# A fused retention and two-layer MLP kernel: a shorter path for the decay factors, and a new order of the opening

## The chip, the cores and the metric

The kernel runs on one core of a Trainium2 chip. The metric is the device time of one execution in microseconds (us); the kernel before takes 575.96 us, the median of three runs (574.5 to 576.0). The core has five engines that run side by side, each with its own queue in program order: TensorE (PE), which multiplies matrices into PSUM, VectorE (DVE), ScalarE (ACT), GpSimd (POOL) and SyncE (SP), which here issues most of the DMAs. TensorE has its own row for weight loads (PEld). On-chip memory is SBUF, 128 partitions wide; PSUM has 8 banks, and a bank holds one 128x512 float32 tile.

## The reference

Inputs are q, k, v of shape 2 x 8 x 768 x 64 (batch, heads, positions, head size), one decay factor lam for each of the 8 heads, and five weight matrices. The first part is a retention (linear attention with decay), here with all of it in one formula for a chunk of positions b:

```
intra = ((q_b k_b^T) * lam^(i-j) for j <= i, else 0) @ v_b
inter = (q_b * lam^(i+1)) @ state
out_b = intra + inter
state = lam^n * state + (k_b * lam^(n-1-j))^T @ v_b        # n positions in a chunk
```

Its result, as 1536 tokens x 512, goes through a first MLP (`h = x @ w_in`, `g = relu(h)^2`, `g @ w_out`, width 2048) and a second one (`gate = sigmoid(x @ w_gate)`, `val = x @ w_val`, `(gate * val) @ w_out`, width 1536). All of it is float32.

## The kernel before

The kernel takes chunks of 128 positions: chunks 0 to 5 are those of the first sequence, 6 to 11 those of the second, and `PAIRS` (line 22) couples chunk n with chunk n + 6. A pair needs these steps: `att_scores` (L368, 8 small float32 matmuls that show as 16 instructions) for each chunk; `att_mask` (L423, DVE), which multiplies the scores by the decay mask `D`; `query` (L376, POOL), which multiplies q by the rows `L` of decay powers; `att_keys` (L384, POOL) or `keys_by_act` (L392, ACT), which scale k by the column `W`; `att_out` (L463 with the state, L475 with the values); `att_uv` (L447), the product of keys and values, and `att_state` (L487, L489), which adds it to the state `S`; `decayed` (L429, POOL) is the state times `G`. For chunks 0 and 6 the scaled keys are made another way: `turn_keys` (L402) transposes the loaded k on TensorE with the identity matrix `same`, and `turned_keys` (L412, DVE) scales the result.

`decays` (L271 to L318) builds the factors at the start. lam comes by one DMA that writes the 8 values to all 128 partitions (L269, on the SP queue). DVE and ACT spread it to 512 columns (L296), two scans on DVE (L298) make `D`, and `W` follows (L302). `rows(r)` multiplies `D` by a column on TensorE so that its last row stands in all partitions (L311), and ACT copies the result to `L` (L316). `decay_of_state` (L320) makes `G` on POOL. Before the first real matmul, `warm_up(14)` (L331) runs 14 matmuls of 128x512 on zeros.

The MLP matmuls need each float32 operand as a high and a low part, so a weight goes through a chain: load (L139, SP), two scalings on ACT (L153, L157, the word "a" of the plan), shift and add on DVE (L164, L169, "j"), high part by ACT ("h") or DVE ("H", both L230), low part on DVE (L237, "l"). `stage_a` (L538, 12 matmuls) makes h for one f of 16, `elem` and `split_g` (ACT L569, L570, L582, and DVE L584, "g") work on it, `stage_b` (L552, 12 matmuls) multiplies by w_out.

The order of the work is written out by hand. `OPENING` (line 18) is a list of words, one call each, from the scores of chunk 0 to the scores, outputs and states of the first two pairs; the numbers are chunks, and for o and u pairs (R rows, T turned keys, d their scaling, s scores, m mask, q query, K keys, x copy of the result to its high part, z its low part on DVE, o output, u state product, y state, t decayed state). Then `step_1(f)` runs for f = 0 to 15: stage_a(f), stage_b(f - 1), with the letters of `PLAN[f]` between them. Each step has two halves, half 2f after stage_a(f) and half 2f + 1 after stage_b(f - 1); `SLOTS` (line 24) says at which half the scores and outputs of pairs 2 to 5 run on TensorE, and `LOADS` (line 25) at which half the SP queue issues the loads of their q, k and v. Later stages (second MLP, store) are not touched by the change.

Of the kernel before, what the change touches and what calls it, by code (L numbers as in the profile page):

```python
# [12 lines left out]
P = 128  # L13
CH = 128
TB = 512
WARM = 14
SINGLE = 10
OPENING = "R0 T0 s0 R1 m0 q7 s6 q1 q8 T6 m6 d6 a d0 j o0 u0 x0 s1 s7 y K7 x6 m1 h m7 K1 G t z0 l o1 a x1 x7 z6 z7 j a z1 H l j H u1 l".split()
PLAN = ('ga|ajhjlaHl', '|jagajHlH', 'aljg|hjH', '|llqgKmkaj', 'Hqlaa|jhlg', 'jmq|gamKhlajmqj', 'Hmklg|aj', 'aghl|mKakm', 'jhq|aqjglq', 'jhml|gamjqajhm', 'mgla|jh', 'gl|hhlhm', 'lgl|', 'g|', 'g|', '|g')
# [4 lines left out]
SLOTS = ((7, 'scores', 2), (8, 'scores', 8), (10, 'out', 2), (11, 'scores', 3), (12, 'scores', 9), (14, 'out', 3), (16, 'scores', 4), (17, 'scores', 10), (19, 'out', 4), (20, 'scores', 5), (21, 'scores', 11), (23, 'out', 5))  # L24
LOADS = {10: 'v9 v3', 4: 'q2 q9', 20: 'v11', 5: 'q3 q10', 17: 'q5 q12 v5', 1: 'v2 v8', 12: 'v4 q11 q4 v10'}
# [7 lines left out]
def retention_moe_kernel(  # L33
# [80 lines left out]
    def load_kv(c, eng=nc.sync):  # L114
        t = kv_t[c] = double("kv")
        n = c in PAIRS[0]
        eng.dma_start(out=t[:, n:], in_=kv[c, :, n:].rearrange("s t h d -> s t (h d)"))
# [132 lines left out]
    lam8 = const.tile([P, H, 1], F32, name="lam8")  # L250
    seen = const.tile([P, 1], F32, name="seen")
    W = const.tile([P, H, 1], F32, name="W")
    lam_half = const.tile([P, 2, 4, 1], F32, name="lam_half")
# [3 lines left out]
    G = const.tile([P, 2, 4, 1], F32, name="G")  # L257
# [9 lines left out]
    def load_lam():  # L267
        src = bass.AP(lam.tensor, lam.offset, [[0, P], [1, H]])
        nc.sync.dma_start(out=lam8[:, :, 0], in_=src)  # L269

    def decays():  # L271
# [4 lines left out]

        nc.vector.memset(warm, 0.0)
# [9 lines left out]
        nc.vector.tensor_scalar(  # L287
# [5 lines left out]
        )  # L293
        lam_r = pairs_of(lam8)
        for r, copy in enumerate((nc.vector.tensor_copy, nc.scalar.copy)):
            copy(step_d[:, r, :, 1:], lam_r[:, r].to_broadcast([P, 4, CH - 1]))  # L296
        for r in range(2):
# [4 lines left out]
        nc.vector.tensor_tensor(  # L302
            out=pairs_of(W), in0=lam_r, in1=D[:, :, :, CH - 1 :], op=ALU.mult
        )
        last = spot_d[:, 0, 0, 0:1].to_broadcast([P, 64])
        row_t = [bank(), bank()]

        def rows(r):

            for s in range(2):  # L310
                nc.tensor.matmul(  # L311
                    row_t[s][half(r ^ s)], lhsT=last, rhs=D[:, r], start=True, stop=True
                )
            if r:
                for s in (1, 0):
# [1087 lines left out]
```

## Time and profile before

| | |
|---|---|
| median of 3 runs | 575.96 us (574.5 to 576.0) |
| profiled execution, its own time | 574.55 us |
| its span, first to last instruction | 572.4 us |
| TensorE busy | 567.6 us, 99% of the span |
| DVE, ACT, POOL busy | 442.0, 350.3, 53.2 us |
| mean DMA rate | 262 GB/s |
| chain that ended last | PE 98%, DVE 1% |

The profile is of one execution, taken by the hardware profiler; its times are counted from the span's start. Busy shares of TensorE are modelled, so the chain of waits and the start times of the matmuls say more than they do. A view by lines names the line of the kernel, the engine, the operation and its tiles ("out<-in"); "xN" is the count of instructions.

### The profile page before, as it was taken

To read this page: it belongs to the slowest core of one execution; us is meant where nothing else is said; L and a number is where in the kernel's file an instruction comes from. 1 tells how busy PE (TensorE), PEld (TensorE's weight loads), DVE (VectorE), ACT (ScalarE), POOL (GpSimd) and SP (SyncE) were. 2 spreads that over 40 slices of the span, in tenths; PEclk is the share of its full clock that TensorE was granted. 3 is DMA by queue.
4 is the path that set the end of the run, shared out by engine and by line. 5 is a ranking of instruction groups with operands and counts; after the bars stand their busy time and mean duration, and the time that the engine had idled before them with its cause. 6 is when DMAs were issued, how large, how long until landed. Compare 5 with 4: busy or idle time off the path is not lost.

```text
span 572.4 us, 8640 instructions
## 1 busy us (share of the span) xinstructions
PE 567.6 (99%) x3050; PEld 464.2 (81%) x3050; DVE 442.0 (77%) x653; ACT 350.3 (61%) x569; POOL 53.2 (9%) x54
## 2 busy tenths in 40 slices
PE   9999999999999999999999999999999999999997
PEld 5878788888888888888888888888888888888885
DVE  5998887967788867765656778884778887789966
ACT  3688898867565467674648565544555555475552
POOL 3313613000000000000000000120011112000110
PEclk9999999999999999999999999999999999999999
DMA  8999998211454499999985899983546669599681
GB/s 305 407 407 413 408 352 302 93 38 37 148 183 148 148 360 347 408 412 409 405 322 187 304 342 346 370 261 71 159 84 171 225 193 252 189 345 340 212 289 74
DMA packets 68843, 149.74 MB, mean 262 GB/s; under 512 B 6976, under 2 KB 15168, under 8 KB 68800
## 3 DMA queue, kind: packets, MB, share of 16 engines
q1 hardware_dynamic: 64448, 141.59, 67.6%
q0 software_dynamic: 3840, 6.69, 6.0%
q10 hardware_dynamic: 512, 0.92, 0.5%
q8 instruction: 24, 0.39, 0.3%
q14 instruction: 19, 0.16, 0.1%
HBM read 105.39 MB, written 42.21 MB: 258 GB/s over the span
## 4 chain that ended last, share of the span: by engine, by line
PE 98%; DVE 1%; DVEq 0%; issue 0%
PE p L747 33%; PE p L538 19%; PE p L1145 15%; PE p L552 14%; PE p L1074 10%; PE p L368 2%; PE p L475 2%; PE p L331 1%; PE p L447 1%; PE p L463 1%; DVE xl L507 0%; DVE at L423 0%; PE p L311 0%; PE p L402 0%; DVE wlo L237 0%; DVE j L169 0%
## 5 line engine op out<-in xcount | busy, mean ns | idle before, releaser
L747 PE MATMUL p<-xch,ah 128*128 128x512 f32 x280 | 109.1, 390 | 0.0
L747 PE MATMUL p<-xcl,ah 128*128 128x512 f32 x280 | 109.0, 389 | 0.0
L747 PE MATMUL p<-xch,al 128*128 128x512 f32 x280 | 108.9, 389 | 0.0
L757 ACT COPY s<-p 128x512 f32<-128x512 f32 x60 | 35.2, 586 | 68.3 <-PE p L747 68.3
L747 PEld LDWEIGHTS p<-xch,ah 128*128 128x128 f32 x280 | 52.5, 188 | 11.3 <-ACT s L757 0.3
L747 PEld LDWEIGHTS p<-xch,al 128*128 128x128 f32 x280 | 52.6, 188 | 11.0
L747 PEld LDWEIGHTS p<-xcl,ah 128*128 128x128 f32 x280 | 52.6, 188 | 10.9
L1074 PE MATMUL p<-gq,wq 128*128 128x512 f32 x252 | 57.5, 390 | 0.0
L1074 PEld LDWEIGHTS p<-gq,wq 128*128 128x128 f32 x252 | 47.2, 188 | 10.1 <-DVE wq L1031 0.3
L169 DVE CUSTOM_DVE_ANT_0 j<-j,r 128x1024 uint16<-128x1024 uint16 (+1 forms) x57 | 46.6, 817 | 5.8
L1145 PE MATMUL p<-g2h,whi 128*128 128x512 f32 x128 | 49.8, 389 | 0.0
L1145 PE MATMUL p<-g2l,whi 128*128 128x512 f32 x128 | 49.8, 389 | 0.0
L1145 PE MATMUL p<-g2h,wlo 128*128 128x512 f32 x128 | 49.8, 389 | 0.0
L153 ACT ACTIVATE j<-raw 128x512 f32<-128x512 f32 x68 | 45.7, 672 | 5.9 <-DMA raw<-in_w 2.0
L157 ACT ACTIVATE r<-raw 128x512 int32<-128x512 uint32 x68 | 45.3, 666 | 1.5 <-PE p L538 1.0
L762 DVE TENSOR_TENSOR c<-p,s 128x512 f32<-128x512 f32 x60 | 41.2, 687 | 5.7 <-PE p L747 4.1
L538 PE MATMUL p<-xh,whi 128*128 128x512 f32 x160 | 43.7, 395 | 0.0
L538 PE MATMUL p<-xl,whi 128*128 128x512 f32 x160 | 42.9, 390 | 0.1
L538 PE MATMUL p<-xh,wlo 128*128 128x512 f32 x160 | 43.0, 390 | 0.0
L695 POOL DMA_DIRECT2D as<-w x6 | 5.6, 928 | 354.6 <-DMA u<-w 278.6
L538 PEld LDWEIGHTS p<-xl,whi 128*128 128x128 f32 x160 | 30.0, 188 | 6.8 <-DVE xl L507 0.5
L538 PEld LDWEIGHTS p<-xh,wlo 128*128 128x128 f32 x160 | 30.0, 188 | 6.6 <-DVE wlo L237 0.3
(133 smaller groups left out, 1027.1 us busy)
## 6 DMA issues: line engine op xcount, KB each, us to landing
raw<-in_w SPq DMA_DIRECT2D x68, 512.0 KB, 7.6
w<-j SPq DMA_DIRECT2D x68, 256.0 KB, 7.1
u<-w SPq DMA_DIRECT2D x52, 256.0 KB, 5.5
a<-w SPq DMA_DIRECT2D x20, 512.0 KB, 4.1
g<-g SPq DMA_DIRECT2D x32, 256.0 KB, 4.0
g<-g SPq DMA_DIRECT2D x16, 512.0 KB, 7.6
gr<-gs SPq DMA_DIRECT2D x24, 256.0 KB, 5.3
qk<-in_qk SPq DMA_DIRECT2D x11, 512.0 KB, 7.7
```

The costliest lines, as they stand in the source:

```text
L153: lambda: nc.scalar.activation(j, t[:, :, 1].bitcast(F32), AF.Prelu, scale=2.0**-80 if flip else 2.0**-112, alpha=2.0**-32 if flip else 2. ...
L157: lambda: nc.scalar.activation(r, low, AF.Copy, scale=2.0**-29),
L169: nc.vector.tensor_tensor(out=j, in0=j, in1=r, op=ALU.add)
L368: nc.tensor.matmul(pv(sc[g])[:, p, :], lhsT=pv(t[:, 1, :])[half(g), p, :], rhs=pv(t[:, 0, :])[half(g), p, :], start=True, stop=True,)
L475: nc.tensor.matmul(ov[s][half(r), p, :], lhsT=v[:, 2 * p + r, :], rhs=pv(at[:, r ^ s, :])[:, p, :], start=n == 0 and p == 0, stop=p == 3, ...
L538: nc.tensor.matmul(acc, lhsT=a[:, kk * P : (kk + 1) * P], rhs=b[:, kk, :], start=i == 0, stop=i == 11,)
L552: nc.tensor.matmul(acc[e], lhsT=a[:, e * P : (e + 1) * P], rhs=b, start=first and i == 0, stop=last and i == 2,)
L747: nc.tensor.matmul(acc, lhsT=w[:, col, kk * P : (kk + 1) * P], rhs=x[:, kk, :], start=start and i == 0, stop=stop and i == 5, skip_group_c ...
L757: nc.scalar.copy(s, acc)
L762: nc.vector.tensor_tensor(out=c, in0=acc, in1=s, op=ALU.add)
L1074: nc.tensor.matmul(acc[k], lhsT=a[:, wn], rhs=block_of(b, gn), start=first and n == 0, stop=last and n == 3 * len(group) - 1,)
L1145: nc.tensor.matmul(acc[e, t], lhsT=a[:, e * P : (e + 1) * P], rhs=b[:, t, :], start=first and i == 0, stop=last and i == 2,)
```

## The change

lam is loaded as one row of 8 values by the ACT queue (before the load of q and k of chunk 6), while the load of q and k of chunk 0 becomes the first of the SP queue. A matmul with a column of ones spreads the row over the partitions into a PSUM bank, and DVE copies it from there. The warm-up is split: 4 matmuls before that small matmul, 5 behind it. `same` is made on POOL. The matmuls of `rows` and the ACT copies are gone; POOL builds `L` by doubling: it copies lam to column 0 and then, in seven steps, multiplies the n columns that exist by the n-th to get n more. `G` is the last column of `L`, so `decay_of_state` is gone; `W` is copied from `D`. In the opening the words stand in a new order, and in the loads v0 comes ahead of q7 and the second weight ahead of v1 and v7. In `SLOTS` the two chunks of a pair have their scores at one half for pairs 2, 4 and 5, and those of chunk 3 stand behind the outputs of pair 2 (12 halves with attention work become 8), and `LOADS` has four places where it had seven. In `out_now` the outputs come ahead of the state products. In `PLAN` three high parts move from ACT to DVE (9 h and 9 H for 12 and 6), and one scaling of keys from POOL to ACT (4 k and 2 K for 3 and 3).

```diff
--- before.py
+++ after.py
@@ -13,16 +13,16 @@
 P = 128
 CH = 128
 TB = 512
-WARM = 14
+WARM = 4, 5
 SINGLE = 10
-OPENING = "R0 T0 s0 R1 m0 q7 s6 q1 q8 T6 m6 d6 a d0 j o0 u0 x0 s1 s7 y K7 x6 m1 h m7 K1 G t z0 l o1 a x1 x7 z6 z7 j a z1 H l j H u1 l".split()
-PLAN = ('ga|ajhjlaHl', '|jagajHlH', 'aljg|hjH', '|llqgKmkaj', 'Hqlaa|jhlg', 'jmq|gamKhlajmqj', 'Hmklg|aj', 'aghl|mKakm', 'jhq|aqjglq', 'jhml|gamjqajhm', 'mgla|jh', 'gl|hhlhm', 'lgl|', 'g|', 'g|', '|g')
+OPENING = "s0 q1 a T0 m0 q7 q8 s6 T6 m6 d6 s1 K1 o0 d0 j K7 x6 u0 s7 y x0 m1 m7 o1 h a l t x1 x7 z6 a z0 z7 z1 j H l j H u1 l".split()
+PLAN = ('g|ajajahlH', '|ljgajHlaa', 'Hjlh|gjHl', '|lgamjqKHak', 'a|ljgHqlq', 'gjm|mmhklmaa', 'jHlkq|agjj', 'h|lamKag', 'mhjjgl|kHajqqq', 'lm|hgamaqmmh', 'jjaHgl|', 'jgl|lhmhll', 'g|', 'g|', 'g|', '|g')
 QUERIES = (2, 9, 3, 10, 4, 11, 5, 12)
 
 PAIRS = ((0, 6), (1, 7), (2, 8), (3, 9), (4, 10), (5, 11))
 LEAD = 2
-SLOTS = ((7, 'scores', 2), (8, 'scores', 8), (10, 'out', 2), (11, 'scores', 3), (12, 'scores', 9), (14, 'out', 3), (16, 'scores', 4), (17, 'scores', 10), (19, 'out', 4), (20, 'scores', 5), (21, 'scores', 11), (23, 'out', 5))
-LOADS = {10: 'v9 v3', 4: 'q2 q9', 20: 'v11', 5: 'q3 q10', 17: 'q5 q12 v5', 1: 'v2 v8', 12: 'v4 q11 q4 v10'}
+SLOTS = ((7, 'scores', 2), (7, 'scores', 8), (10, 'out', 2), (10, 'scores', 3), (11, 'scores', 9), (14, 'out', 3), (15, 'scores', 4), (15, 'scores', 10), (18, 'out', 4), (19, 'scores', 5), (19, 'scores', 11), (22, 'out', 5))
+LOADS = {13: 'v4 q11 q4 v10', 3: 'v2 v8 q2 q9', 8: 'q3 q10 v9 v3', 16: 'q5 q12 v5 v11'}
 
 MM = 0.2267
 SCORES = 1.0
@@ -113,7 +113,7 @@
 
     def load_kv(c, eng=nc.sync):
         t = kv_t[c] = double("kv")
-        n = c in PAIRS[0]
+        n = f"T{c}" in OPENING
         eng.dma_start(out=t[:, n:], in_=kv[c, :, n:].rearrange("s t h d -> s t (h d)"))
 
 
@@ -248,13 +248,13 @@
 
 
     lam8 = const.tile([P, H, 1], F32, name="lam8")
+    lam_row = const.tile([1, H], F32, name="lam_row")
+    ones = const.tile([1, P], F32, name="ones")
     seen = const.tile([P, 1], F32, name="seen")
     W = const.tile([P, H, 1], F32, name="W")
-    lam_half = const.tile([P, 2, 4, 1], F32, name="lam_half")
     warm = const.tile([P, P], mybir.dt.bfloat16, name="warm")
     D = const.tile([P, 2, 4, CH], F32, name="D")
     L = const.tile([P, 2, 4, CH], F32, name="L")
-    G = const.tile([P, 2, 4, 1], F32, name="G")
     same = const.tile([P, P], F32, name="same")
     S = const.tile([P, 2, 4, 64], F32, name="S")
 
@@ -265,8 +265,14 @@
         return t.rearrange("a (p r) o -> a r p o", r=2)
 
     def load_lam():
-        src = bass.AP(lam.tensor, lam.offset, [[0, P], [1, H]])
-        nc.sync.dma_start(out=lam8[:, :, 0], in_=src)
+        src = bass.AP(lam.tensor, lam.offset, [[0, 1], [1, H]])
+        nc.scalar.dma_start(out=lam_row, in_=src)
+
+    def spread_lam():
+
+        t = bank()
+        nc.tensor.matmul(t[:, 0:H], lhsT=ones, rhs=lam_row, start=True, stop=True)
+        nc.vector.tensor_copy(lam8[:, :, 0], t[:, 0:H])
 
     def decays():
 
@@ -274,6 +280,7 @@
 
 
 
+        nc.vector.memset(ones, 1.0)
         nc.vector.memset(warm, 0.0)
         step_d, spot_d = (
             double(name).rearrange("a r (p b) -> a r p b", p=4) for name in ("step_d", "spot_d")
@@ -284,13 +291,16 @@
         nc.gpsimd.iota(across, pattern=[[1, P]], base=0, channel_multiplier=-1)
         nc.scalar.copy(seen, warm[:, 0:1])
         nc.vector.memset(step_d[:, :, :, 0:1], 0.0)
-        nc.vector.tensor_scalar(
+        nc.gpsimd.tensor_scalar(
             out=same, in0=across, scalar1=0.0, scalar2=None, op0=ALU.is_equal
         )
         nc.vector.tensor_scalar(
             out=spot_d.rearrange("a r p b -> a (r p) b"), in0=shift,
             scalar1=float(CH - 1), scalar2=None, op0=ALU.is_equal,
         )
+        warm_up(WARM[0])
+        spread_lam()
+        warm_up(WARM[1])
         lam_r = pairs_of(lam8)
         for r, copy in enumerate((nc.vector.tensor_copy, nc.scalar.copy)):
             copy(step_d[:, r, :, 1:], lam_r[:, r].to_broadcast([P, 4, CH - 1]))
@@ -299,30 +309,23 @@
                 *(t[:, r].rearrange("a p b -> a (p b)") for t in (D, step_d, spot_d)),
                 initial=0.0, op0=ALU.mult, op1=ALU.add,
             )
-        nc.vector.tensor_tensor(
-            out=pairs_of(W), in0=lam_r, in1=D[:, :, :, CH - 1 :], op=ALU.mult
-        )
-        last = spot_d[:, 0, 0, 0:1].to_broadcast([P, 64])
-        row_t = [bank(), bank()]
-
-        def rows(r):
-
-            for s in range(2):
-                nc.tensor.matmul(
-                    row_t[s][half(r ^ s)], lhsT=last, rhs=D[:, r], start=True, stop=True
-                )
-            if r:
-                for s in (1, 0):
-                    nc.scalar.copy(L[:, s].rearrange("a p b -> a (p b)"), row_t[s])
-
-        return rows
-
-    def decay_of_state():
+        nc.vector.tensor_copy(pairs_of(W), D[:, :, :, CH - 1 :])
+
+    def rows():
+
+
+
         lam_r = pairs_of(lam8)
-        nc.gpsimd.tensor_copy(lam_half[half(0)], lam_r[half(0)])
+        nc.gpsimd.tensor_copy(L[half(0), :, :, 0:1], lam_r[half(0)])
         for s in range(2):
-            nc.gpsimd.tensor_copy(lam_half[half(1), s], lam_r[half(1), 1 - s])
-        nc.gpsimd.tensor_tensor(out=G, in0=lam_half, in1=L[:, :, :, CH - 1 :], op=ALU.mult)
+            nc.gpsimd.tensor_copy(L[half(1), s, :, 0:1], lam_r[half(1), 1 - s])
+        n = 1
+        while n < CH:
+            nc.gpsimd.tensor_tensor(
+                out=L[:, :, :, n : 2 * n], in0=L[:, :, :, 0:n],
+                in1=L[:, :, :, n - 1 : n].to_broadcast([P, 2, 4, n]), op=ALU.mult,
+            )
+            n *= 2
 
     def warm_up(n):
 
@@ -428,7 +431,8 @@
         t = unit("tt")
         eng.tensor_tensor(
             out=t.rearrange("a (n e) -> a n e", n=8), in0=S.rearrange("a s p e -> a (s p) e"),
-            in1=G.rearrange("a s p o -> a (s p) o").to_broadcast([P, 8, 64]), op=ALU.mult,
+            in1=L[:, :, :, CH - 1 :].rearrange("a s p o -> a (s p) o").to_broadcast([P, 8, 64]),
+            op=ALU.mult,
         )
         tt_t.append(t)
 
@@ -1175,8 +1179,8 @@
         pair = PAIRS[k]
         if k < SEQ_CH - 1:
             decayed()
+        att_out(pair)
         att_uv(pair)
-        att_out(pair)
         passed(REST)
 
         def after():
@@ -1200,13 +1204,13 @@
         "h": lambda: couple_high(nc.scalar.copy), "H": lambda: couple_high(nc.vector.tensor_copy),
         "l": couple_low, "q": lambda: query(queries.pop(0)),
         "k": lambda: keys_by_act(keys_left.pop(0)), "K": lambda: att_keys(keys_left.pop(0)),
-        "G": decay_of_state, "t": decayed, "y": att_state,
+        "t": decayed, "y": att_state,
     }
 
-    def opening(rows):
+    def opening():
         one = {
-            "R": rows, "s": att_scores, "T": turn_keys, "d": turned_keys, "q": query,
-            "m": att_mask, "K": att_keys, "x": att_x, "z": low_x,
+            "s": att_scores, "T": turn_keys, "d": turned_keys, "q": query,
+            "m": att_mask, "K": att_keys, "k": keys_by_act, "x": att_x, "z": low_x,
             "o": lambda n: att_out(PAIRS[n]), "u": lambda n: att_uv(PAIRS[n]),
         }
         for what in OPENING:
@@ -1269,13 +1273,14 @@
     T5 = T4 + (12 + 42 * NF2) * MM
 
     with tc.manual_schedule():
+        load("q0")
         load_lam()
         load("q6", nc.scalar)
-        load("q0 q7 v0 w q1 v6 q8 v1 v7 w w w w w")
-        rows = decays()
-        warm_up(WARM)
+        load("v0 q7 q1 w v6 q8 w v1 v7 w w w w")
+        decays()
+        rows()
         new_xr()
-        opening(rows)
+        opening()
         clock[0] = 0.0
         flush()
```

## Rows read from the trace of the kernel before

**Rows 1.** Chain of waits in order of time, opening to 46 us: start us, us, what.

```profile
0.99 5.37 PE p L331 x14
6.36 1.01 PE p L311 x4
...
27.21 2.72 PE p L552 x12
29.93 3.03 PE p L538 x12
...
41.14 1.09 PE p L368 x16
42.23 2.95 PE p L538 x12
```

**Rows 2.** Timeline, all engines, 0 to 22 us: start, duration, engine, line, idle before.

```profile
3.56 0.42 DVE L296 COPY step_d<-lam 128x508 f32<-128x508 f32 x1 [0.67 <-DMA lam<-in_lam]
4.02 2.34 DVE L298 TENSOR_TENSOR_SCAN D<-step_d,spot_d 128x512 f32<-128x512 f32 x2
7.30 1.11 PE L402 MATMUL p<-same,qk 64*128 64x64 f32 x16
11.08 3.75 POOL L376 TENSOR_TENSOR qd<-qk,L 128x512 f32<-128x512 f32 x3 [9.05 <-ACT L L316]
15.56 2.28 POOL L384 TENSOR_TENSOR kd<-kv,W 128x512 f32<-128x512 f32 x2 [0.74 <-DMA kv<-in_kv]
17.21 1.10 PE L463 MATMUL p<-qd,S 64*64 64x128 f32 x32
17.79 0.18 POOL L322 COPY lam_half<-lam 64x8 f32<-64x8 f32 x1
17.98 0.69 ACT L153 ACTIVATE j<-raw 128x512 f32<-128x512 f32 x1 [1.05 <-DMA raw<-in_w]
18.41 0.21 POOL L325 TENSOR_TENSOR G<-lam_half,L 128x8 f32<-128x8 f32 x1
21.08 1.20 PE L538 MATMUL p<-xh,whi 128*128 128x512 f32 x4
```

**Rows 3.** Waits from 0 to 30 us: who waited for whom, us, times, longest.

```profile
PEld p L538 <- DVE xl L507: 0.5, 1, 0.5
```

**Rows 4.** DMA issues of 1.17 to 1.61 us: count, KB each, us to landing.

```profile
qk<-in_qk SPq DMA_DIRECT2D x1, 512.0 KB, 5.1
```

**Rows 5.** DMA packets of the window 1.1 to 3.5 us.

```profile
DMA packets 177, 0.14 MB, mean 58 GB/s; under 512 B 144, under 2 KB 144, under 8 KB 177
```

**Rows 6.** Windows of 1 us: length, busy by engine, TensorE clock, DMA share, GB/s.

```profile
5.00:6.00 1.00, 1.00 (x6) 0.35 (x3) 1.00 (x2) 0.00 (x0) 0.00 (x0) 1.00 0.99 393
```

**Rows 7.** Timeline of 23 to 33 us, ACT and PE.

```profile
24.52 0.60 ACT L569 ACTIVATE r<-p 128x512 f32<-128x512 f32 x1 [2.54 <-PE p L538]
...
26.35 0.67 ACT L153 ACTIVATE j<-raw 128x512 f32<-128x512 f32 x1
...
27.50 0.66 ACT L153 ACTIVATE j<-raw 128x512 f32<-128x512 f32 x1
...
29.05 0.63 ACT L230 CAST whi<-j 128x512 fp32r<-128x512 f32 x1 [0.33 <-DVE j L169]
...
32.79 1.09 PE L552 MATMUL p<-gh,whi 128*128 128x512 f32 x4
```

**Rows 8.** Windows of 5 us, columns as in group 6.

```profile
30.00:35.00 5.00, 5.00 (x22) 3.78 (x22) 4.69 (x10) 4.94 (x10) 0.00 (x0) 1.00 1.02 407
```

**Rows 9.** Timeline of 41 to 48 us: ACT and DVE.

```profile
41.36 2.02 ACT L392 ACTIVATE kd<-kv,W 128x64 f32<-128x64 f32 x8 [0.74 <-DMA w<-j]
...
47.13 1.41 DVE L230 CAST whi<-j 128x512 fp32r<-128x512 f32 x1
```

**Rows 10.** DMA issues of 35 to 40 us, and SP's own waits from 20 to 130 us.

```profile
qk<-in_qk SPq DMA_DIRECT2D x2, 512.0 KB, 8.3
...
SPq L117 <- ACT r L157: 4.8, 1, 4.8
```

## The prediction

> **What bounds the kernel now.** I read the page first: TensorE is 99% of the chain, so only three things can move the time: when TensorE starts its dense work, how much work it has, and where it waits. The chain in order of time shows where it is not dense [rows 1]. It begins with 14 warm-up matmuls (0.99 us, 5.37 long), then small float32 matmuls in a row, then a stretch led by DVE, and from 23.3 us on nothing but PE pieces, 2.72 us for 12 matmuls (0.227 each). In that stretch there is one slow group of 12 (3.03 instead of 2.72, at 29.93) and an extra 0.23 us wherever 12 matmuls follow a piece of attention (2.95 instead of 2.72, at 42.23). The timeline of the opening comes next [rows 2]: what was TensorE, or its operands, late for? Last come the waits [rows 3]: 0.5 us for the low part of x is the only one on weights of the main matmuls.
>
> So the time is the start of the first main matmul (21.08 us, rows 2), plus fixed work behind it, plus a few gaps. The profiled execution took 574.55 us, span 572.4, so 2.15 lie around the span. It is the fastest of the shown runs but for rounding: their median is 1.41 above it.
>
> **Term 1, the start of the dense work.** The rows matmuls go: two groups of four, 1.01 us each [rows 1], 2.02 us. The spread of lam adds one tiny matmul (its nearest row is 0.25 us, a quarter of such a group; it lies inside the warm-up). The 14 warm-ups take 5.37 us, 0.38 each, so 9 take 3.5; the wait for lam stands between them. Here lam, a broadcast to 128 partitions, landed at about 3.5: the copy at 3.56 waited for it [rows 2]. As one row at the head of another queue it lands no later than that and after its issue (about 1.1); with this broadcast the nearest row, I take 2.8. The five later warm-ups then end at about 5.0, and D comes as before, at 6.4 (copy 0.42, scans 2.34, rows 2, begun about 0.1 earlier, less the new copy).
>
> The next matmuls are the scores of chunk 0, which need q0 and not D. In the kernel before q0 landed at 1.18 + 5.1 = 6.3 [rows 4]. Ahead of it on the same queue stood lam's small packets: 144 packets below 512 bytes from 1.1 to 3.5 us, in which all queues moved 58 GB/s [rows 5]; later the same engines moved 393 GB/s [rows 6]. Now q0 is first: at best 512 KB at 393 GB/s from 2.0 us on, 3.4; at worst it is only issued 0.44 earlier (0.74 for 1.18) and lands at 5.8. I take 4.8, so these scores begin at 5.3.
>
> From there the same matmuls as before run to the first main one: before from 7.30 to 21.08 with one rows group inside, 13.78 - 1.01 = 12.77 us without a wait [rows 1, 2]. So 5.3 + 12.77 = 18.1, if data keeps up. D at 6.4 is not late: the mask of chunk 0 is wanted by the first output, which stands behind five of these pieces of about 1 us, at 10.
>
> L is next late? The doubling is three copies (0.18 each) and seven products. The 128x8 product took 0.21 and the 128x512 one 1.28 at most [rows 2], so 1.65 to 2.1 ns an element: 7 x 0.2 + 1016 elements x 1.65 to 2.1 = 3.1 to 3.5, with the copies 3.6 to 4.0. L is there at 7.4 instead of 11, and the three queries (1.25 each, 3.75 in all) end by 11.2, or by 13.2 should q8 land late; the state part of output 1 wants them at 14.2 (before it began 21.08 - 17.21 = 3.9 us ahead of the first main matmul, rows 2). Hidden; without that cover it is 4 us.
>
> The loads decide. v1 and v7 have a weight more ahead of them (512 KB, 1.3 us at 393 GB/s). v7 landed at 15.5: POOL waited for it until 15.56 [rows 2]. The queue starts between 0.4 us earlier (the issue) and 1.5 (lam's packets gone from 2.0 to 3.5), I take 1.0, so v7 lands at 15.8, its scaled keys are ready at 17.0 (1.14 each, rows 2), and the last state product (1.1, as the other groups of small matmuls) ends at 18.1. Both paths meet; I take 18.5, between 17.8 and 20.2. The gain is 21.08 - 18.5 = 2.6 us, between 0.9 and 3.3.
>
> **Term 2, from there to the second MLP group.** Before, the L552 group of f = 1 began 32.79 - 21.08 = 11.71 us after the first main matmul [rows 2, 7]. Now the plan puts three "a" ahead of the high part of weight 4. Counted from the first main matmul: relu at 3.04 (the third group of four begins at 1.81, and relu came 1.23 behind it), 1.83 to the first "a", three at 1.15, the high part 0.63 [rows 7]: 8.95, then 12 matmuls, 2.72: 11.67. The two small waits go (0.5 for the low part of x, 0.31 for that of a weight) and one of 0.8 us (8.95 less three groups of 12, 8.16) for a high part comes. Sum: 0.0, between -0.4 and +0.8.
>
> **Term 3, fewer changes of kind.** Attention stands at 8 places instead of 12. Each place costs the 12 matmuls behind it 0.23 us [rows 1]. That is 4 x 0.23 = 0.9, which I take; if the cost comes with each piece and not with each place, it is 0. That outputs now stand ahead of state products moves no work.
>
> **Term 4, the conversions at a faster pace.** From 30 to 35 us ACT is busy 4.94 and DVE 4.69 of 5.00 us [rows 8]: TensorE 2.6 us earlier wants its weights 2.6 us earlier. They start earlier too (the copies of L on ACT are gone, and the masks come with the scores, 2 us sooner). In the plan ACT gains one scaling of keys (2.02, rows 9) and gives up three high parts (0.63 or, of two weights, twice that), about even; DVE takes these, and a DVE cast beside a POOL product took 1.41 us [rows 9]. TensorE's gaps from that lie between 0 and 2.5 us; I take 0.6.
>
> **Sum.** -2.6 + 0.0 - 0.9 + 0.6 = -2.9: 571.65 us against the profiled execution. The shown median is 1.41 above that execution and one run of three is at it, so I put 1.0 on top: **572.6 us**.
>
> **Rivals.**
> *The opening waits for data.* The weight that landed behind v7 came 2.4 us after it (ACT waited until 17.98, rows 2), not 1.3. If that step now lies ahead of v7, it lands at 17.9 less at most 1.0, its keys are ready at 18.5 to 19.2, and the dense work starts at 19.7 to 20.2: gain 0.9 to 1.4, with terms 3 and 4 1.2 to 1.7 in all; with the 1.0 on top, 573.9 to 574.4. For it: the rate of the queue is the limit through the whole opening. Against: the queue starts earlier.
> *TensorE starts at its low clock.* The warm-ups average 0.38 us against 0.227 for the same 512 columns later [rows 1], so most ran at the lower of the two levels (1.2 GHz), although the granted clock reads 1.00 in every row [rows 6, 8]. Nine with a pause for lam may not raise it; if the first 3 us of scores take twice as long, term 1 is +0.4 instead of -2.6, and the time is 575.6. The Trainium skill ("TensorE: Matmul & The Clock Gate", What's actually happening) has the low level as the default that sustained work lifts; by it the pause is a danger, and the trace of before, which has none there, can't say.
> *POOL starts late.* POOL now makes `same` and the products of L. On the chip here its first copy took 0.18 us with nothing ahead of it, at 17.79 [rows 2], so I price first calls at nothing. If `same` came at 8.1, 6 us late, T0 (wanted at 6.3) would lose 1.8 us and L, at 12, nothing more: gain 0.8 + 0.9 - 0.6, 574.4 with the 1.0. The Trainium skill ("GPSIMD Engine Reference", 2.1 Instruction dispatch) gives about 6 us for the first call of a freshly loaded kernel, which would do that; the row speaks against it.
> *Slower: q and k arrive after their slot.* q3 and q10 are now issued at half 8 for half 10, q4 and q11 at 13 for 15. Between issue and use lie about 9.6 us of TensorE (2.95 + 2.72 + the 3.9 of a pair's outputs and state). Loads took 8.3 us there, and SP once stood 4.8 us for a buffer [rows 10]. Up to 1.3 us of lateness is free; at 4.8 at both places TensorE loses 2 x 3.5 = 7.0 us, against a gain of 3.5 from terms 1 and 3: 574.55 + 3.5 + 1.0 = 579.0. It decides from 3.0 us of lateness at each. Against it: the queue has fewer weights ahead at those points.
>
> **Chances.** The forecast 0.58, its own range 570.3 to 574.2; data-bound opening 0.16; low clock 0.07; late POOL 0.04; late q and k 0.10; a larger gain 0.05. The range for 8 in 10 is 570.0 to 576.2. About 0.3% (1.7 us) is what can be told from no change: below 574.2 counts as faster. That takes the forecast, the larger gain and a third of the data-bound case: 0.68; slower, above 577.7, 0.10; the rest, 0.22, the same.
>
> **What would show it.** Right: no matmul between the warm-ups and the scores; scores of chunk 0 near 5.3; first L538 near 18.5; v7's keys last before it; a gap of 0.8 us ahead of the fourth weight's matmuls; 12 matmuls at 2.95 us eight times, not twelve. Wrong: TensorE waiting on same, L or lam for over 1 us, matmuls of the scores at twice their length, or gaps ahead of scores at halves 10 and 15.

## The result, and the profile after

The kernel after takes 571.28 us (median of four executions, 570.67 to 571.48), the kernel before 575.98 beside it: a ratio of 0.9917 [0.9891, 0.9943]. The forecast was 572.6. The profiled execution took 571.35 us (before 574.55): its span is 569.6 (572.4), and 1.75 us lie around it (2.15). TensorE has 11 matmuls fewer:

```profile
PE 562.7 (99%) x3039; PEld 463.7 (81%) x3039; DVE 445.7 (78%) x657; ACT 348.1 (61%) x572; POOL 58.2 (10%) x60
...
PE 95%; DMA 3%; ACT 1%; issue 0%; ACTq 0%; DVE 0%; DVEq 0%; SPq 0%
```

These are the busy times and the shares of the chain on the page of after. Of the chain that ended last 3% are now DMA, where before it was all TensorE and DVE. Next comes that chain in order of time (start us, us, what), from the start to 62 us:

```profile
1.28 6.58 DMA qk<-in_qk
...
8.24 9.56 DMA kv<-in_kv
...
17.93 1.09 PE p L479 x16
19.03 0.93 PE p L451 x32
19.96 2.97 PE p L542 x12
...
28.16 0.61 ACT whi L230
...
28.82 3.04 PE p L542 x12
...
40.02 1.99 PE p L371 x32
42.00 2.95 PE p L542 x12
...
51.42 1.90 PE p L479 x32
53.32 0.93 PE p L451 x32
```

Until 17.8 us the chain is loads: q6, issued by ACT at 1.28, for whose landing at 7.85 SP held back the issue of v1 and v7 (e4 shows below that this hold is not what makes v1 late), then v7, which landed at 17.80 and released the second half of output 1. From there it is TensorE with one gap, ahead of weight 4. Two sets of scores at one place are 1.99 us (before twice 1.09 at two places, each followed by 12 matmuls at 2.95, [rows 1]), and the state product behind the outputs takes 0.93. The timeline of the opening of after (start, duration, engine, line, idle before):

```profile
3.45 1.99 PE L334 MATMUL p<-warm 128*128 128x512 bf16 x5
...
4.21 2.34 DVE L308 TENSOR_TENSOR_SCAN D<-step_d,spot_d 128x512 f32<-128x512 f32 x2
4.27 2.27 POOL L321 COPY L<-lam 64x4 f32<-64x4 f32 x2
...
5.36 1.16 PE L371 MATMUL p<-qk 64*128 64x128 f32 x16
...
6.62 3.47 POOL L324 TENSOR_TENSOR L<-L 128x8 f32<-128x8 f32 x7
...
8.60 1.23 PE L371 MATMUL p<-qk 64*128 64x128 f32 x16 [1.23 <-DMA qk<-in_qk]
...
16.71 2.49 POOL L387 TENSOR_TENSOR kd<-kv,W 128x512 f32<-128x512 f32 x2 [2.50 <-DMA kv<-in_kv]
...
17.93 1.09 PE L479 MATMUL p<-at,kv 128*64 128x128 f32 x16 [0.22 <-DMA kv<-in_kv]
...
19.89 1.19 PE L542 MATMUL p<-xh,whi 128*128 128x512 f32 x4
```

The scores of chunk 0 start at 5.36 (forecast 5.3), behind the last warm-up; those of chunk 6 wait 1.23 us for q7, and output 1 waits for v7. The first main matmul starts at 19.89, not at 21.08 [rows 2], and not at the forecast 18.5. q0 was not late. This is its row among the DMA issues of 0.70 to 0.75 us (count, KB, us to landing), where before it took 5.1 [rows 4]:

```profile
qk<-in_qk SPq DMA_DIRECT2D x1, 512.0 KB, 3.3
```

It landed at 0.73 + 3.3 = 4.0. What slowed behind it shows in windows of 1 us of after (length, busy by engine PE, PEld, DVE, ACT, POOL, then clock, DMA share, GB/s):

```profile
2.00:3.00 1.00, 1.00 (x4) 0.16 (x2) 0.57 (x1) 1.00 (x1) 0.88 (x2) 1.00 0.94 340
3.00:4.00 1.00, 1.00 (x4) 0.70 (x5) 0.41 (x2) 0.56 (x3) 0.21 (x1) 1.00 0.86 225
4.00:5.00 1.00, 1.00 (x4) 0.30 (x2) 0.97 (x2) 0.37 (x1) 0.96 (x2) 1.00 0.67 205
```

From 2 us on the loads run at 340 GB/s, then fall to 205 to 270 until 7 us; before they were at 393 at 5 us [rows 6]. By 8 us both kernels had brought in as much (1.73 and 1.76 MB): the early start of the queue was used up.

Where the 3.2 us come from, in the profiled executions: first main matmul -1.19; from there to the L556 group of f = 1 (L552 before) +0.09; from that group to the first matmul of the stage that follows (L751, L747 before; at 129.90 and 132.92 us) -1.92; behind it +0.2; around the span -0.4.

### The profile page after: what moved, and what is told of

The parts are those of the page before. It is cut to its first block, busy times and chain, and to the rows that moved or that the text cites. A ratio compares the mean times of both kernels' runs of the same rounds, so it can differ in the third digit from the quotient of the medians.

```text
span 569.6 us, 8628 instructions
## 1 busy us (share of the span) xinstructions
PE 562.7 (99%) x3039; PEld 463.7 (81%) x3039; DVE 445.7 (78%) x657; ACT 348.1 (61%) x572; POOL 58.2 (10%) x60
## 4 chain that ended last, share of the span: by engine, by line
PE 95%; DMA 3%; ACT 1%; issue 0%; ACTq 0%; DVE 0%; DVEq 0%; SPq 0%
PE p L751 33%; PE p L542 19%; PE p L1149 15%; PE p L556 13%; PE p L1078 10%; DMA kv<-in_kv 2%; PE p L479 2%; PE p L371 1%; DMA qk<-in_qk 1%; PE p L467 1%; PE p L451 1%; ACT j L153 0%; ACT r L157 0%; ACT g L574 0%; ACT whi L230 0%
## 5 line engine op out<-in xcount | busy, mean ns | idle before, releaser
L751 PE MATMUL p<-xch,ah 128*128 128x512 f32 x280 | 109.1, 390 | 0.0
L751 PE MATMUL p<-xcl,ah 128*128 128x512 f32 x280 | 109.0, 389 | 0.0
L751 PE MATMUL p<-xch,al 128*128 128x512 f32 x280 | 108.9, 389 | 0.0
L751 PEld LDWEIGHTS p<-xch,ah 128*128 128x128 f32 x280 | 52.6, 188 | 11.5 <-ACT s L761 0.3
L751 PEld LDWEIGHTS p<-xch,al 128*128 128x128 f32 x280 | 52.6, 188 | 10.9
L751 PEld LDWEIGHTS p<-xcl,ah 128*128 128x128 f32 x280 | 52.6, 188 | 10.8
L169 DVE CUSTOM_DVE_ANT_0 j<-j,r 128x1024 uint16<-128x1024 uint16 (+1 forms) x57 | 47.8, 839 | 6.0 <-DVE j L164 0.5
L542 PEld LDWEIGHTS p<-xh,whi 128*128 128x128 f32 x160 | 29.5, 188 | 7.3 <-ACT whi L230 0.9
```

The source lines that it names most:

```text
L169: nc.vector.tensor_tensor(out=j, in0=j, in1=r, op=ALU.add)
L542: nc.tensor.matmul(acc, lhsT=a[:, kk * P : (kk + 1) * P], rhs=b[:, kk, :], start=i == 0, stop=i == 11,)
L751: nc.tensor.matmul(acc, lhsT=w[:, col, kk * P : (kk + 1) * P], rhs=x[:, kk, :], start=start and i == 0, stop=stop and i == 5, skip_group_c ...
```

## The experiments

"First main" is the start of the first main matmul in the timeline, "next stage" that of the first L751 in the chain of waits, both of the profiled execution. Before has 21.08 and 132.92.

| run | median us | ratio to before | profiled us | first main | next stage |
|---|---|---|---|---|---|
| after | 571.28 | 0.9917 [0.9891, 0.9943] | 571.35 | 19.89 | 129.90 |
| e1_opening_only | 573.23 | 0.9977 [0.9963, 0.9992] | 573.51 | 19.87 | 132.19 |
| e2_middle_only | 572.94 | 0.9966 [0.9949, 0.9983] | 572.61 | 21.00 | 131.42 |
| e3_states_first | 571.29 | 0.9941 [0.9922, 0.9959] | 571.47 | 19.92 | 130.31 |
| e4_q6_by_sp | 571.52 | 0.9943 [0.9926, 0.9959] | 571.45 | 20.20 | 130.13 |
| e5_values_first | 570.99 | 0.9941 [0.9922, 0.9959] | 570.95 | 19.26 | 129.52 |
| e6_lam_to_all | 575.25 | 1.0019 [1.0002, 1.0037] | 575.67 | 22.68 | 134.19 |
| e7_no_warm | 573.16 | 0.9988 [0.9965, 1.0012] | 572.52 | 21.28 | 131.28 |
| e8_first_column_by_dve | 571.73 | 0.9952 [0.9935, 0.9970] | 571.60 | 19.93 | 130.06 |
| e9_weight4_early | 570.74 | 0.9926 [0.9911, 0.9942] | 571.61 | 20.27 | 130.30 |
| e10_pause_early | 570.51 | 0.9930 [0.9917, 0.9944] | 570.74 | 19.20 | 129.48 |
| e11_three_more | 570.95 | 0.9939 [0.9926, 0.9951] | 571.12 | 19.25 | 129.51 |
| e12_copies_first | 570.66 | 0.9928 [0.9913, 0.9942] | 572.13 | 19.41 | 130.82 |

Before, beside these runs, had medians of 574.42 to 574.92.

**The opening and the middle, each alone.** The first run has after's opening with before's middle, the second the reverse.

```diff
 e1: -PLAN, SLOTS, LOADS, out_now (outputs first) of after
     +PLAN, SLOTS, LOADS, out_now (state products first) of before
 e2: the opening, its loads and the decay factors of before; the four above of after
```

> The changed kernel with the slots, loads, plan and the order of states and outputs of the kernel before: only the opening is changed. Theory (the parts add up: the first main matmul comes 1.2 us earlier, at about 19.9, and nothing behind it is lost): 1.2 us below the kernel before, 573.3 to 573.4 in the profiled run. Rival (the old plan's conversions can't follow an earlier start, so the new plan is needed for it): no more than 0.3 us below the kernel before, with gaps of 0.5 us or more on TensorE between 28 and 45 us.

> The kernel before with only the slots, loads, plan and order of outputs and states of the changed one. Theory (fewer changes of kind 4 x 0.23, score sets in a row 3 x 0.19, state products behind outputs 3 x 0.15, no new gap): 1.9 us below the kernel before, 572.6 in the profiled run; first main matmul at 21.1 as before. Rival (the prediction's two terms: 0.9 for places and 0.6 lost to conversions): 0.3 us below. Second rival (the plan only fits the new opening): above the kernel before, with gaps on TensorE ahead of scores or weights.

The opening alone brings 1.0 us (profiled; 1.3 in medians), the middle alone 1.9 (1.6); together 2.9, of the 3.2 that the whole change brings. The parts add up, as the theories of both runs had it. In e1 the old middle gives 0.48 us of the earlier start back: from the first main matmul to the next stage it takes 112.32 us, in before 111.84. Three pieces of its chain are longer than in before, where they take 3.03, 2.72 and 2.72:

```profile
28.63 3.23 PE p L542 x12
...
34.60 2.81 PE p L542 x12
...
48.23 2.97 PE p L542 x12
```

In the chain of e2 the stretch from 33.38 to 131.42 us is 98.04, to the hundredth that of after (31.86 to 129.90); before it was 99.96. Its own piece of scores is that of after:

```profile
33.38 2.72 PE p L552 x12
...
41.53 1.99 PE p L368 x32
...
54.84 0.93 PE p L447 x32
```

**State products ahead of the outputs, as before.**

```diff
-        att_out(pair)
         att_uv(pair)
+        att_out(pair)
```

> The changed kernel with the state products ahead of the outputs again in the four later pairs. Theory: each of three state products takes 1.08 us instead of 0.93, 0.45 us above the changed kernel (571.8 where that takes 571.35). Rival (the prediction: the order moves no work): the same within 0.1 us on the chain of waits, with 1.08 us shared out elsewhere.

The chain of e3 shows the 0.15 us a pair that the forecast had put at nothing: 1.08 here for 0.93, three times.

```profile
50.42 1.08 PE p L451 x32
```

The next stage is 0.41 us later than in after, near the 0.45 of the theory. The medians (571.29 and 571.28) don't resolve it.

**What slows the loads: q6 by the other queue, or the order.**

```diff
 e4:     load("q0"); load_lam()
-        load("q6", nc.scalar)
+        load("q6")
 e5: -        load("v0 q7 q1 w v6 q8 w v1 v7 w w w w")
     +        load("q7 v0 q1 w v6 q8 v1 v7 w w w w w")
```

> The changed kernel with the load of q and k of chunk 6 on the SP queue, behind that of chunk 0, and only lam's row on the ACT queue. Theory (that load on the second queue is starved, lands at 7.9 and also holds up the issue of v1 on SP until then): q6 lands near 5, q7 by 7.0, the scores of chunk 6 start at 7.4 instead of 8.6, v7 lands 1.5 to 2.5 us earlier, first main matmul at 18.3 to 18.6 instead of 19.9, and the time is 1.2 to 1.6 us below the changed kernel (569.8 to 570.2). Rival (the engines move only 205 to 270 GB/s from 4 to 7 us for a reason of their own): the rate stays, q7 lands at 8 or later, gain at most 0.3 us.

> The changed kernel with q7 ahead of v0 and the second weight behind v1 and v7 in the first loads, as the order of the kernel before had it. Theory (the changed opening is bound by landings: q7 at 8.5 holds the scores of chunk 6, v1 and v7 at 16.6 and 17.8 hold output 1 and its states): q7 lands at about 7.9, v7 at about 16, the first main matmul starts at 18.6 to 19.0 instead of 19.9, the time is 0.9 to 1.3 us below the changed kernel. Rival (the second weight is then late, as it landed at 17.9 before, and the chain over ACT and DVE to the second group of matmuls takes the place): first main matmul earlier, but a gap ahead of the second group of 12, gain under 0.3 us.

The theory of e4 failed. SP issued v1 1.9 us earlier than in after (5.97 for 7.87), yet v1 landed at 17.0 (16.6 in after), and the slow stretch was still there, only later (180 and 213 GB/s from 4 to 6 us), as v0 was one place later in the queue. It has another cause of a late start too: in its timeline the first matmuls take twice as long (1.00 from the start of these scores to the next start in after, 1.87 here), so its time does not tell the price of the loads alone.

```profile
5.69 2.08 PE L371 MATMUL p<-qk 64*128 64x128 f32 x16
7.56 1.81 PE L405 MATMUL p<-same,qk 64*128 64x64 f32 x16
```

e5, with q7 ahead of v0 and v1 and v7 ahead of a weight, has no wait of TensorE for a load. Its windows of 1 us:

```profile
3.00:4.00 1.00, 1.00 (x4) 0.70 (x5) 0.41 (x2) 0.56 (x3) 0.22 (x1) 1.00 1.03 365
4.00:5.00 1.00, 1.00 (x4) 0.30 (x2) 0.96 (x2) 0.36 (x1) 0.96 (x2) 1.00 0.99 389
```

The rate is 365 and 389 GB/s where after has 225 and 205, and the dip (252) comes at 5 to 6 us. So in these three runs it follows the place of v0; why the loads are slow there stays open. The first main matmul gains 0.63 us, the profiled execution 0.4, less than the 0.9 to 1.3 of the theory; the medians differ by 0.3, which the scatter of e5 (570.61 to 573.49) doesn't resolve. The chain of e5 says what took the place of the loads, DVE from 9.27 us on:

```profile
11.86 1.14 DVE j L164
...
13.13 1.54 DVE j L169
...
18.25 2.39 DVE xl L511 x4
```

The shift and add of a weight takes 1.14 + 1.54 beside POOL's queries and keys, 0.42 + 0.69 without them (22.81 and 23.37 us of the same run). In before the add of this weight fell into a pause of POOL (14.83 to 15.56) and took 0.69. That POOL is the cause is argued from this coincidence in time; no run takes POOL's work away there.

```profile
15.25 0.69 DVE L169 CUSTOM_DVE_ANT_0 j<-j,r 128x1024 uint16<-128x1024 uint16 x1
```

**lam by a broadcast again, on the ACT queue.**

```diff
-        src = bass.AP(lam.tensor, lam.offset, [[0, 1], [1, H]])
-        nc.scalar.dma_start(out=lam_row, in_=src)
+        src = bass.AP(lam.tensor, lam.offset, [[0, P], [1, H]])
+        nc.scalar.dma_start(out=lam8[:, :, 0], in_=src)
-        spread_lam()
```

> The changed kernel with lam again written to all 128 partitions by its DMA, on the ACT queue, and no spreading matmul. Theory (lam's row by itself brings little; q0's place at the head of the SP queue does): lam is there at about 3.5, D within 0.3 us of now, time within 0.3 us of the changed kernel. Rival (the small packets hold up all transfers as in the prediction's first term): q7 lands 1 us or more later than 8.5, the time is 0.8 to 1.2 us higher.

The theory of e6 failed. All that after gains is lost, more than the rival had priced: first main at 22.68, 2.79 us later than in after. The waits of e6 from 0 to 30 us:

```profile
DVE step_d L305 <- DMA lam<-in_lam: 4.1, 1, 4.1
...
PE p L370 <- DMA qk<-in_qk: 3.3, 2, 2.2
```

lam lands at 6.7 us (issued at 0.72, 6.0 to landing), and the other loads with it are slow: 144, 177 and 135 GB/s in the windows from 2 to 5 us, where after has 340, 225 and 205. The scores of chunk 6, which wait for q7, start at 10.41 instead of 8.60: 1.8 of the 2.79 us. Behind it a second thing costs time, TensorE's clock: the column of the granted clock falls to 0.58, 0.50, 0.50 and 0.71 in the windows from 12 to 16 us, after TensorE had stood idle for 1.13 and 2.15 us, and the scores of chunk 1 took 2.03 us (1.18 in after). A window and that row of the timeline:

```profile
13.00:14.00 1.00, 1.00 (x14) 1.00 (x10) 1.00 (x4) 1.00 (x2) 0.92 (x2) 0.50 1.03 422
12.33 2.03 PE L370 MATMUL p<-qk 64*128 64x128 f32 x16
```

Another 1.5 us goes between the first main matmul and the next stage, with one wait of 1.4 us for a mask of DVE. One row and a matmul of 8 columns in place of 128 small rows is the part of the opening without which, in this run, nothing comes off.

**No warm-up matmuls.**

```diff
-        warm_up(WARM[0])
         spread_lam()
-        warm_up(WARM[1])
```

> The changed kernel without the nine warm-up matmuls. Theory (the scores of chunk 0 start at about 4.2, when q0 lands, and take twice as long at the lower clock, and the wait for q7 at 8.5 hides that; the clock then rises later): scores of chunk 6 and what follows are slow for 2 to 4 us, time 0.5 to 1.5 us above the changed kernel. Rival (the opening is bound by landings alone, and warm-ups buy nothing): the same within 0.3 us.

The theory holds in the profiled execution. The timeline of e7: lam's row has landed at 2.05, the scores of chunk 0 start 1.4 us earlier than in after, and take twice as long, as do those of chunk 6 (8.89 us).

```profile
2.05 0.56 PE L274 MATMUL p<-lam_row,ones 1*128 1x8 f32 x2 [2.05 <-DMA lam_row<-in_lam]
4.00 2.08 PE L369 MATMUL p<-qk 64*128 64x128 f32 x16 [1.38 <-DMA qk<-in_qk]
5.87 1.81 PE L403 MATMUL p<-same,qk 64*128 64x64 f32 x16
```

The first main matmul comes at 21.28. So the warm-up is worth 1.2 us (profiled; 1.9 in medians, with ten times from 572.41 to 578.63).

**The first column of L by DVE.**

```diff
-        nc.gpsimd.tensor_copy(L[half(0), :, :, 0:1], lam_r[half(0)])
+        nc.vector.tensor_copy(L[half(0), :, :, 0:1], lam_r[half(0)])
   (and the two of the other half)
```

> The changed kernel with the three copies of lam to the first column of L on DVE, behind its two scans, so that POOL does nothing while the scans run. Theory A (the POOL copies that stand from 4.27 to 6.54 beside the scans are also what holds the DMAs at 205 to 270 GB/s from 4 to 7 us): the rate is 340 GB/s or more there, q7 lands by 7.7, time 0.6 to 0.9 us lower. Theory B (the rate has to do with the transfers themselves, the 2 KB rows of v0 and the 64 rows of q6): the rate and the time stay, L comes 0.4 us later, which nothing waits for.

Theory B's outcome came, though not the cause it names: the copies, behind the scans, took 0.16 and 0.24 us in the timeline of e8, and the rate of the loads stayed low (199 GB/s from 4 to 5 us). POOL's waiting copies are not what slowed the loads, and their 2.3 us cost after nothing that shows (first main 19.93 for 19.89).

```profile
6.67 0.16 DVE L319 COPY L<-lam 64x8 f32<-64x8 f32 x1
6.84 0.24 DVE L321 COPY L<-lam 64x4 f32<-64x4 f32 x2
```

**The gap ahead of weight 4.** On top of e5:

```diff
-PLAN = ('g|ajajahlH', ...
+PLAN = ('gajah|lajH', ...
```

> The run with q7 ahead of v0 in the loads, and PLAN[0] = 'gajah|lajH' for 'g|ajajahlH': the shift and add of the fourth weight stand ahead of the state add on DVE, and its high part ahead of the third scaling pair on ACT. In the run without this edit the f = 2 group of L542 began at 28.37 us, 0.34 behind the end of the group ahead of it (weights waited 0.76 for ACT's high part and 0.30 for DVE's low part), and the 12 matmuls took 3.17 us instead of 2.72. Theory (the middle's last gap is only an order on ACT and DVE): the high part ends near 27.6 instead of 28.32, the group starts at 28.0, its low part (behind the state add, near 29.0) is in time, so 0.3 + 0.3 to 0.45 us come off: 570.3 to 570.4 us beside the 570.95 of that run's profiled execution. Rival (DVE is the limit in this stretch): the state add in front of the low part, and the shift and add of the next weight behind it, make the next group of 12 late by as much, and the first L751 of f = 14 stays at 129.5 (+-0.15): 570.8 to 571.0 us.

The gap ahead of weight 4 is gone: in the timeline of e9 the group of f = 2 follows without a wait. But its profiled execution had the slow scores of e4, with the same times (5.69 and 7.56), and began the dense work 1.0 us later than e5 with the same instructions up to there.

```profile
28.60 1.09 PE L542 MATMUL p<-xh,whi 128*128 128x512 f32 x4
```

From the first main matmul to the next stage it took 110.03, e5 110.26. These 0.23 us don't come from the edit alone, since the conversions had 1.0 us more before the dense work began. The next two runs have the same plan and start the dense work as early as e5 (19.20 and 19.25 for 19.26). In both the group of f = 2 follows without a wait, and yet the next stage comes at 129.48 and 129.51, where e5 has 129.52: the time comes back as waits for conversions, in e10 ahead of the group of f = 3:

```profile
27.71 1.07 PE L542 MATMUL p<-xh,whi 128*128 128x512 f32 x4
...
33.87 1.20 PE L542 MATMUL p<-xh,whi 128*128 128x512 f32 x4 [0.31 <-DVE whi L230]
```

So the rival holds: with this opening the conversions are the limit of the stretch, and this order only moves the gap.

**Where the warm-up pauses, and how long it is.** On top of e9:

```diff
-WARM = 4, 5
+WARM = 2, 7        # e10
+WARM = 4, 8        # e11
```

> The run with q7 ahead of v0 and the fourth weight early, with 2 + 7 warm-up matmuls where it had 4 + 5: the spread of lam stands between the second and the third. Of that run the profiled execution (571.61) had the scores of chunk 0 at 1.87 us and T0 at 1.60, and the first main matmul at 20.27; its execution times fell in two groups, 570.6 to 570.8 and 571.6. Theory (the level of the clock at the scores of chunk 0 is what parts the two groups, and a longer unbroken stretch of warm-ups behind the spread raises it in time): spread at 2.1 us, seven warm-ups to 5.0 to 5.6, scores of chunk 0 at 5.6 or before in about 1.0 us and T0 in 0.84, first main matmul near 19.2, no time of 571.5 or above, median 570.2 to 570.6. Rival (the level does not hang on where the pause stands): scores of chunk 0 at 1.3 to 1.9 us in the profiled execution or times in two groups again, median 570.7 (+-0.2).

> The run with q7 ahead of v0 and the fourth weight early, with 4 + 8 warm-up matmuls where it had 4 + 5. Theory (the level rises under the warm-ups): three more of them, 0.22 to 0.43 us each, put the scores of chunk 0 at 6.3 to 7.0 us instead of 5.69, but all of them at the upper level (1.0 us, T0 0.84); against the best opening seen (first main matmul at 19.26) that is 0.6 to 1.0 later, 19.9 to 20.3, and the times fall in one group, 571.2 to 571.6. Rival (the dense work has slack there, since it hangs on DVE or on the loads): first main matmul at 19.3 to 19.6, 570.6 to 570.9. If the scores still take 1.3 us or more, the level does not hang on the number of warm-ups.

The five times of e10 lie in one group (570.26 to 570.74) and its median is the lowest of all, 570.51. Of the theory the times and the first main matmul came out, the level did not: the scores of chunk 0 still began at half speed (1.24 us to the next start), the rest ran at full speed. In e12, with the same warm-ups, they took 1.82, so the place of the pause does not set the level. The timeline of e10:

```profile
5.69 1.41 PE L371 MATMUL p<-qk 64*128 64x128 f32 x16
...
19.20 1.20 PE L542 MATMUL p<-xh,whi 128*128 128x512 f32 x4 [0.73 <-ACT xh L503]
```

In e11 all scores run at full speed (0.99), from 5.92 on: the three added warm-ups cost 0.23 us. Yet in e5, e10 and e11 the first main matmul stands at 19.26, 19.20 and 19.25, though output 0 began at 10.93, 10.60 and 10.58. TensorE is not what sets it any more: DVE (e5, e11) is, and in e10 ACT, behind the load of the second weight, which landed at 16.9. The rival of e11 holds.

**The copies of the results ahead of a weight's scaling.** On top of e10:

```diff
-... m7 o1 h a l t x1 x7 z6 a z0 ...
+... m7 o1 h l t x1 x7 a z6 a z0 ...
```

> The run with 2 + 7 warm-ups, with the copies of the two last results to their high parts (x1, x7) ahead of the second weight's scaling pair in the list of the opening. In the run without this edit the last state product ended at 18.4 us, but the first main matmul began at 19.20: ACT had waited until 16.91 for the second weight's load and made its scaling pair before the copies, which ended at 19.16 (output 1 had been ready at 17.5). Theory (an order on ACT): the copies end at 18.5, the first main matmul starts at 18.6, and the conversions behind it move with it: 0.5 to 0.6 us off, median 569.9 to 570.0, first L751 of f = 14 at 128.9. Rival (the conversions of the weights have become the bound, as the fourth term of the forecast had it): the first main matmul starts earlier, but the scaling pairs and DVE's shift and add don't, gaps open between 22 and 34 us, and the time stays at 570.4 to 570.6, first L751 at 129.4.

The run decides nothing: its six times reach from 569.79, the lowest of any run, to 572.13. The profiled execution is the slowest of them. It had 1.82 us for the scores of chunk 0, and a wait of 0.7 us for a mask of DVE at 42.2, which of the other runs only e6 has (1.4); from the waits of TensorE from 34 to 60 us:

```profile
PE p L542 <- DVE at L426: 0.7, 1, 0.7
```

Whether the faster ones lack both stays open.

## Why the prediction was right, and which terms were not

The forecast (572.6, faster) holds, but by luck in part: in the sum, -2.9 forecast and -3.2 measured in the profiled executions, two errors of about 1.5 us cancel (term 1 too high, terms 3 and 4 too low), and a third put 1.0 on top.

**Term 1, the start of the dense work: 1.2 us gained, 2.6 forecast.** The failed step is the landing of v7: 15.8 forecast, 17.8 measured, 2.3 us later than in before (15.5). I had let the queue's earlier start (1.0 us) run through to v7; but the loads ran at 205 to 270 GB/s from 3 to 7 us, and the start was used up by 8 us. That is half of the 2.0. The other half is the weight that now stands ahead of v7, priced at 1.3 us by its 512 KB at 393 GB/s: it cost 2.3, though the loads ran at 418 GB/s from 8 us to v7's landing (412 in before). They brought in 4.1 MB in that time, 3.1 in before, so almost 0.5 MB besides this weight came in ahead of v7's end; of which loads is not shown. That is the first rival's opening, almost to the number (v7 at 16.9 to 17.9, first main at 19.7 to 20.2), and its price for the weight, 2.4. D came as forecast (6.55 for 6.4), and so did the scores of chunk 0, though with q0 at 4.0 instead of 4.8 it was the warm-ups that set their start.

The 18.5 would not have been met with v7 in time either: e5, e10 and e11 stop at 19.2. The step "12.77 us of matmuls from the scores on" left out the other engines, though the prediction's first paragraph names a stretch led by DVE: in e5 and e11 DVE, whose shift and add of a weight beside POOL takes 2.7 us instead of 1.1, and in e10 ACT, which waited for a weight until 16.91 and scaled it ahead of the copies of the results.

L was later than forecast (10.1 for 7.4) without a wait of TensorE for it, as its cover promised. The products took 3.47 us (3.1 to 3.5 forecast). It was the small copies: forecast 0.18 each, the last two took 2.27 together, until the end of the scans on DVE. In before two POOL copies of the same size, with no scan beside them, took 0.31:

```profile
18.02 0.31 POOL L324 COPY lam_half<-lam 64x4 f32<-64x4 f32 x2
```

The Trainium skill ("SBUF — State Buffer", "SBUF: two separate sides") has a port pair that VectorE and GpSimd share, held for the whole instruction, and names VectorE operations with two SBUF inputs among those that lock GpSimd out. The trace agrees: the scan has two such inputs, and POOL's copies end at 6.54, the scans at 6.55.

**Term 2: 11.80 us, 11.67 forecast.** The gap ahead of weight 4 came as predicted: its group began 8.93 us behind the first main matmul (28.82 less 19.89; 8.95 forecast), with 0.61 for ACT's high part in the chain, and its weight loads had waited 0.9 (0.8 forecast). The 0.13 on top are a wait for the weight's low part, of the kind that was to go: the group took 2.87 us, not 2.72. e9 to e11 show that another order closes this gap, but with an earlier start opens others.

**Terms 3 and 4: 1.92 us gained, 0.3 forecast.** Term 3's four places at 0.23 are there (0.9). The sentence that the new order of outputs and state products "moves no work" failed: it is worth 0.15 a pair, 0.45 in all, of which e3 gives back 0.41. And two sets of scores at one place take 1.99 us, not 2.18: 0.19, three times, 0.57. The sum is 1.9, as measured in after and in e2. The 0.9 and the 0.57 are read from pieces of the chain; no run takes one of them alone. Term 4's gaps (0.6 forecast) did not come in after, since TensorE was 1.2 us earlier and not 2.6. They do come where the opening is faster: e5, e10 and e11 start 0.6 to 0.7 us earlier than after and need 0.25 more to the next stage (110.26 to 110.28 for 110.01), and with before's plan 0.48 go (e1).

**The 1.0 on top** was wrong. The later medians of before are 574.4 to 574.9, at its profiled execution and not 1.4 above it; the three times shown were few. For the same reason the 4.7 us between the two medians of the result are 1.1 to 1.6 too many: the 575.98 is a median of four, and the 3.2 us of the profiled executions are nearer to what the change brings.

**The other rivals.** Late POOL did not happen: `same` took 0.86 us and was ready at 3.0. Late q and k did not: no wait stands ahead of the scores at halves 10 and 15. The low clock did not in the profiled execution of after (1.00 us for the scores of chunk 0), but it does in others of nearly the same program, as below; there it costs about 1.0 us (20.27 in e9 for 19.26 in e5), less than the 3 us of the rival.

## What to carry to other kernels

Where loads set the opening, follow what has landed by a time, not what was issued: after's loads were 1 us ahead at 4 us (0.64 MB, before's stand at 5) and had brought in no more by 8 us, and another order of the loads (e5) started the dense work 0.63 us earlier still. A change of kind on TensorE has a price of its own (here 0.23 us a place, and 0.15 to 0.19 off where like pieces join), and it can be read by adding up pieces of the chain. Before counting on TensorE's own path, sum the other engines over the same stretch, with their durations beside each other and not alone.

## What the runs showed of the hardware

**TensorE's level differs between executions of the same instructions.** In these openings the column of the granted clock reads 1.00 throughout, but the durations tell the level: 0.43 us from one warm-up matmul to the next at first, 0.227 for the same 512 columns later, so 1.2 and 2.4 GHz. In e6 the column does show the lower level (0.50, behind idle stretches of TensorE), so 1.00 in it does not rule that level out. With the same 4 + 5 warm-ups and the pause for lam between them, the scores of chunk 0 took 1.0 us (after, e1, e3), 1.3 (e8), 1.58 (e5) and 1.87 with T0 at 1.60 (e4, e9). e5 and e9 have the same instructions up to 20 us. The times of e9 lie in two groups, 570.6 to 570.8 and 571.6; that the level parts them is argued from the one profiled execution (571.61, low level), not shown. The Trainium skill ("TensorE: Matmul & The Clock Gate", "What's actually happening") says that the point of the rise differs from run to run; these runs agree.

**A load of 128 rows of 32 bytes** took 6.0 us to land beside the large loads of the opening, and these moved 135 to 177 GB/s where they move 205 to 340 without it (e6); in before, at the head of the SP queue, it had landed at about 3.5, 2.8 us from its issue [rows 2]. A single row of 32 bytes was in use at 2.05 (e7).
